# A decode block on one core: TensorE's code in four instruction blocks, VectorE and ScalarE in loops

## The chip, the core and the metric

The kernel runs on one core of one Trainium2 chip. The metric is device time in microseconds (us) of one execution; three runs of the kernel before have a median of 1309.22 us (1309.11 to 1309.62). A core has TensorE (PE in the tables: matrix products; its weight loads are PEld), VectorE (DVE), ScalarE (ACT), GpSimd (POOL) and SyncE (SP, which here only starts transfers), and 16 DMA engines that carry data between the chip's main memory and the core's on-chip memory.

## The reference

The reference is one transformer block that decodes one token for two sequences (B = 2). All numbers are fp32.

```
x: (2, 1, 512)                       k_cache, v_cache: (2, 32 heads, 8192, 128)
q = layernorm(x) @ wq                # wq 512 x 4096 -> 32 heads of 128
p = softmax(q . k_cache / sqrt(128)) # per sequence and head, over 8192 positions
h = x + (p . v_cache) @ wo           # wo 4096 x 512
out = h + (silu(n @ w_gate) * (n @ w_up)) @ w_down,  n = layernorm(h)   # 512 -> 1792 -> 512
```

The two caches are 268 MB each and every byte is used once, so some 565 MB have to be read for about 34 thousand numbers of activations.

## The kernel before, in words

The 64 pairs of a sequence and a head are worked through as 32 units (`U`) of two heads of one sequence. One unit has one K tile and one V tile of 128 partitions by 16384 numbers (8.39 MB): a head's 8192 positions lie over 64 partitions, 128 positions on each. There are two K slots (`kslot`) and one V slot (`vslot`).

For a unit, VectorE multiplies the K tile by the query in two halves (L456) and adds up over the head's 128 numbers (L465), which gives the scores; then it takes each partition's largest score (L473). TensorE turns that column into a row (L355), VectorE takes the largest per head (L409), TensorE spreads it, scaled and negative, over the partitions (L357, L358), ScalarE copies it (L416, `nb`) and computes the exponentials with their sums (L422), TensorE adds the sums over the partitions (L360), VectorE takes the reciprocal (L435). When V has landed, TensorE multiplies it by the probabilities (L365, 32 products in four groups of rows that run beside each other), ScalarE scales and copies (L437, L442), and TensorE and ScalarE bring the unit's result into `oT` (L377, L444). The steps of unit i-1 stand in VectorE's program between the two halves of unit i.

SyncE starts all loads from one list, in order: `wq` (into the V slot), K0 in two halves, K1, V0, K2, V1, K3, and so on, then `wo`, `w_gate`, `w_up` and `w_down` into slots that have come free. A load that overwrites a slot waits until the slot's reader is done (`after`, `freed`): V0 waits for the last product on `wq`, K(i+2) for unit i's sums, V(i+1) for the products on V(i). A load that waits holds up those behind it in the list.

The queries come ahead of the first unit: `xb` holds each normalised input number 64 times, so that a product with 64 columns of weights leaves the query on 64 partitions; 8 groups of products (L328) go by turns into two banks and ScalarE copies each into `qsb` (L339). VectorE's first unit needs the first group alone.

TensorE's 31 first rounds are one loop (`Fori`, L384); VectorE's and ScalarE's programs are written out, unit by unit. TensorE's instructions are fetched in blocks by DMA. At the start TensorE makes a tour: it jumps to `stop1` (L215), and from each of five stops, which stand in different places of its program, to the next (L222) and at last back to `toured`; in the ordinary run each stop is jumped over (L219). After the last unit come `wo`, the second layernorm, gate and up products (L550), the residual (L569: each of four groups of 32 rows of one bank, `f_ps`, begins with a quarter of h), two products whose result nobody reads (L596), and 14 chunks of `w_down`, four products of 128 columns each, added to those four groups (L607). VectorE and ScalarE copy half of the bank each, and two transfers store the result (L634).

Of the kernel before, what the change touches and what calls it, by code (L numbers as in the profile page):

```python
# [5 lines left out]
OP = mybir.AluOpType  # L6
AX = mybir.AxisListType
PE = mybir.EngineType.PE

# [43 lines left out]
def decode_block(nc, x, k_cache, v_cache, wq, wo, w_gate, w_up, w_down, out):  # L53
# [38 lines left out]
    nscale = sbuf("nscale", 1, HP)  # L92
# [5 lines left out]
    om = sbuf("om", P, B, H, NQ)  # L98
# [4 lines left out]
    xT = sbuf("xT", P, DC, B)  # L103
# [21 lines left out]
    nb_ps = bank[0][:, P : P + 1]  # L125
# [12 lines left out]
    s_k = [g.sem(f"k{n}") for n in range(2)]  # L138

# [72 lines left out]
    STOPS = 5  # L212

    def tour(e):
        e.br("stop1")  # L215
        nc.switch_bb("toured", parent=None)

    def place_stop(e, n):
        e.br(f"past{n}")  # L219
        with nc.body(f"stop{n}", parent=None, valid_engines=[PE]):  # L220
            e.nop()
            e.br(f"stop{n + 1}" if n < STOPS else "toured")  # L222
        nc.switch_bb(f"past{n}")

    def stop(n):
        g.steps["tensor"].append(lambda e: place_stop(e, n))
# [22 lines left out]
    do("vector", lambda e: e.tensor_reduce(quarter, ident.rearrange("p (q r) -> p q r", q=NQ), axis=AX.X, op=OP.add))  # L249
    do("vector", lambda e: e.memset(opart, 0.0))  # L250
# [30 lines left out]
    for t, value in (  # L281
# [24 lines left out]
    wait("vector", p)  # L306
    p = do("vector", lambda e: e.tensor_copy(xT, yt), s_dve)  # L307
    wait("vector", p)
    xb = osb.rearrange("p (c m) -> p c m", c=DC * B)
    xb_done = do(  # L310
        "vector",
        lambda e: e.tensor_copy(xb, xT.rearrange("p c b -> p (c b)")[:, :, None].to_broadcast([P, DC * B, HP])),  # L312
        s_dve,
    )
    wait("tensor", xb_done, landed[("wq", 0), 0])
    wqv = vslot.rearrange("p (c m k d) -> p c k m d", c=DC, k=2, d=DH)
    q_done = []
    for n, (m, b) in enumerate((m, b) for m in range(0, MQ, 4) for b in range(B)):
        ps = wide[n % 2].rearrange("p (j d) -> p j d", d=DH)
        if n == 7:  # L320
            stop(1)
        if n > 1:
            wait("tensor", q_done[n - 2])
        for c in range(DC):
            for k in range(2):
                p = do(
                    "tensor",
                    lambda e, ps=ps, c=c, k=k, m=m, b=b: e.matmul(  # L328
                        ps[HALF[k]],
                        xb[:, c * B + b, :],  # L330
                        wqv[:, c, k, m : m + 4, :],
                        start=(c == 0),
                        stop=(c == DC - 1),
                    ),
                    s_pe if c == DC - 1 and k == 1 else None,
                )
        wait("scalar", p)
        q_done.append(
            do("scalar", lambda e, ps=ps, m=m, b=b: e.activation(qsb[:, b, m : m + 4, :], ps, AF.Copy), s_act)  # L339
        )  # L340
    freed["wq", 0] = p
    wait("tensor", consts_done)


    ROUND = 5
    base = g.count[s_pe]

    def at(i, n):
        return s_pe, base + ROUND * i + n

    MROW, NB, DEN, PV, OT = range(1, ROUND + 1)

    def pe_scores(e):
        e.wait_ge(s_dve_pe, 1)
        e.matmul(mrow, m1, ident, start=True, stop=True).then_inc(s_pe, 1)  # L355
        e.wait_ge(s_dve_pe, 2)
        e.matmul(nb_ps[HALF[0]], nscale, gm[:, 0:1], start=True, stop=True)  # L357
        e.matmul(nb_ps[HALF[1]], nscale, gm[:, 1:2], start=True, stop=True).then_inc(s_pe, 1)  # L358
        e.wait_ge(s_act_pe, 1)
        e.matmul(den, sides.rearrange("p w a -> p (w a)"), rs, start=True, stop=True).then_inc(s_pe, 1)  # L360

    def pe_values(e, t_v):
        for w in range(NW):
            t = w % 4
            inst = e.matmul(  # L365
                opart[32 * t : 32 * t + 2 * W, :],
                pz[:, w, :],
                t_v[:, w * W * DH : (w + 1) * W * DH],
                start=(w < 4),
                stop=(w >= NW - 4),  # L370
            )
        inst.then_inc(s_pe, 1)

    def pe_outputs(e):
# [5 lines left out]
        inst.then_inc(s_pe, 1)  # L380

    def pe_rounds(e):
# [9 lines left out]
        place_stop(e, 2)  # L392
# [6 lines left out]
    g.count[s_pe] = at(U - 1, OT)[1]  # L399


    def k_view(i, j0, n):
        return kslot[i % 2][:, j0 * DH : (j0 + n) * DH].rearrange("p (j d) -> p j d", d=DH)

    def biggest(i):
        wait("vector", at(i, MROW))
        do(
            "vector",
            lambda e: e.tensor_reduce(gm, mrow.rearrange("p (k r) -> p k r", k=2), axis=AX.X, op=OP.max),  # L409
            s_dve_pe,  # L410
        )

    def softmax(i):
        s = scores[i % 2]
        wait("scalar", at(i, NB))
        wait("scalar", do("scalar", lambda e: e.activation(nb, nb_ps, AF.Copy), s_act))  # L416
        if i == 0:
            wait("scalar", consts_done)
        for k, h in enumerate(HALF):
            do(  # L420
                "scalar",
                lambda e, k=k, h=h: e.activation(  # L422
                    pz[h, :, k * W : (k + 1) * W],
                    s[h].rearrange("p (w a) -> p w a", a=W),
                    AF.Exp,
                    bias=nb[h],
                    scale=SCALE,
                    accum_out=rs[h],
                ),
                s_act_pe if k else None,  # L430
            )

    def recip(i):
        wait("vector", at(i, DEN))
        p = do("vector", lambda e: e.reciprocal(r, den), s_dve)  # L435
        wait("scalar", p)
        do("scalar", lambda e: e.activation(rdiag, diag, AF.Copy, scale=r))  # L437

    def outputs(i):
        m, b = divmod(i, B)  # L440
        wait("scalar", at(i, PV))
        do("scalar", lambda e: e.activation(osb, opart, AF.Copy), s_act_pe)  # L442
        wait("scalar", at(i, OT))
        return do("scalar", lambda e: e.activation(oT[:, 2 * m : 2 * m + 2, b], ot_ps, AF.Copy), s_act)  # L444

    oT_done = {}
    for i in range(U):
        m, b = divmod(i, B)
        parts = 2
        n = NJ // parts  # L450
        wait("vector", q_done[m // 4 * B + b])
        for c in range(parts):
            wait("vector", landed[("k", i), c if i == 0 else 0])
            kt = k_view(i, c * n, n)
            qb = qsb[:, b, m, :][:, None, :].to_broadcast([P, n, DH])
            mult = do("vector", lambda e, kt=kt, qb=qb: e.tensor_tensor(kt, kt, qb, op=OP.mult), s_dve)  # L456
            if i and c == 0:
                biggest(i - 1)
                softmax(i - 1)
            if i and c == 1:  # L460
                recip(i - 1)
            wait("vector", mult)
            p = do(
                "vector",
                lambda e, kt=kt, s=scores[i % 2][:, c * n : (c + 1) * n]: e.tensor_reduce(s, kt, axis=AX.X, op=OP.add),  # L465
                s_dve,
            )
        freed["k", i] = p
        if i:
            oT_done[i - 1] = outputs(i - 1)  # L470
            freed["v", i - 1] = at(i - 1, PV)
        wait("vector", p)
        do("vector", lambda e, s=scores[i % 2]: e.tensor_reduce(m1, s, axis=AX.X, op=OP.max), s_dve_pe)  # L473
    biggest(U - 1)
    softmax(U - 1)
    do("scalar", lambda e: e.activation(warm, mhalf[:1, :], AF.Sigmoid))
    recip(U - 1)

    zeroed = do("vector", lambda e: e.memset(wide[0], 0.0), s_dve)
    oT_done[U - 1] = outputs(U - 1)
    freed["v", U - 1] = at(U - 1, PV)
    stop(3)
    wait("vector", oT_done[U - 1])
# [21 lines left out]
    wait("tensor", p, zeroed)  # L508
    for c in range(H):
# [54 lines left out]
    stop(4)  # L564
    wait("tensor", h1_done)
    for t in range(4):
        do(
            "tensor",
            lambda e, t=t: e.matmul(  # L569
                f_ps[32 * t : 32 * t + 32, :], place, h1[:, COLS[t] * P : (COLS[t] + 1) * P], start=True, stop=False  # L570
            ),
        )
# [22 lines left out]
    for _ in range(2):  # L595
        do("tensor", lambda e: e.matmul(opart[:32], hT[:, 0, :], osb, start=True, stop=True))  # L596
    wait("tensor", p)
    for c in range(FB):
        if c == 10:
            stop(5)  # L600
# [3 lines left out]
        for t in range(4):  # L604
# [3 lines left out]
                    f_ps[32 * t : 32 * t + 32, :],  # L608
                    gT[:, c * 32 : (c + 1) * 32],
                    wd_t[:, c * D + COLS[t] * P : c * D + (COLS[t] + 1) * P],  # L610
                    start=False,
                    stop=(c == FB - 1),
                ),
                s_pe if c == FB - 1 and t == 3 else None,
            )
    res = rest[:HP, : 2 * P]
# [68 lines left out]
```

## Time and profile before

| | |
|---|---|
| median of three runs | 1309.22 us |
| profiled execution, its own time | 1309.27 us |
| its span (first to last instruction) | 1307.9 us |
| busy: VectorE, TensorE, ScalarE | 1131.1, 433.6, 80.5 us |
| read from main memory | 564.66 MB, 432 GB/s over the span |

The profile's page gives busy time by engine, the span in 40 slices, the DMA queues, and the chain of work that ended last: from the last instruction back to whatever released it, step by step. Such a chain names one reason for each stretch; whether something else would have taken its place has to be read from the stretch itself. Times in the lists of instructions count from the span's start.

### The profile page before, as it was taken

What the parts mean: (1) busy time and instruction counts of PE and PEld (TensorE: products, weight loads), DVE (VectorE), ACT (ScalarE), POOL (GpSimd) and SP (SyncE); (2) the same over time, 40 slices, a digit from 0 to 9 for tenths busy, and PEclk for the clock granted to TensorE, in tenths of its full rate; (3) what the DMA queues carried; (4) which work ended last, traced back from release to release, by engine and by line L of the source; (5) the groups of instructions that cost most, each with busy time, mean ns of one, the idle gap of its engine ahead of it and who ended that gap; (6) DMA issues with size and microseconds to landing.
All of it is one profiled execution on the core that took longest, in us unless ns stands there. A gap on an engine that the chain in (4) does not pass through costs nothing.

```text
span 1307.9 us, 6728 instructions
## 1 busy us (share of the span) xinstructions
PE 433.6 (33%) x2956; PEld 135.5 (10%) x2956; DVE 1131.1 (86%) x246; ACT 80.5 (6%) x272; POOL 3.1 (0%) x15
## 2 busy tenths in 40 slices
PE   1733223333212333322333322333331233332166
PEld 0210001011000011000101100101100010110022
DVE  0999988889888889988888988888998888998841
ACT  0100000000000000000000000000000000000010
POOL 0000000000000000000000000000000000000000
PEclk9965566666566666556666655666665666665689
DMA  9999999999999999999999999999999999999998
GB/s 400 438 439 431 435 435 439 433 433 437 429 437 429 437 429 441 429 439 431 441 433 433 437 429 437 429 439 431 437 429 441 431 437 435 431 437 431 435 423 377
DMA packets 10965, 564.79 MB, mean 432 GB/s; under 512 B 1222, under 2 KB 1226, under 8 KB 1612
## 3 DMA queue, kind: packets, MB, share of 16 engines
q1 hardware_dynamic: 10948, 564.67, 99.7%
q8 instruction: 5, 0.08, 0.0%
q14 instruction: 4, 0.03, 0.0%
q10 hardware_dynamic: 8, 0.01, 0.0%
HBM read 564.66 MB, written 0.00 MB: 432 GB/s over the span
## 4 chain that ended last, share of the span: by engine, by line
DMA 51%; DVE 45%; issue 2%; PE 1%; POOL 0%; SPq 0%; ACT 0%; POOLq 0%; DVEq 0%
DMA kslot<-in_A_k_cache_dram 45%; DVE kslot L456 22%; DVE s L465 22%; DMA kslot<-in_A_v_cache_dram 3%; DMA kslot<-in_B_w_down_dram 3%; PE opart L365 1%; PE wide L328 0%; DVE gm L409 0%; DVE r L435 0%; SPq L627 0%; PE bank L607 0%; PE bank L273 0%; ACT qsb L339 0%; DVE ln_stats L255 0%; POOL ln_rstd L261 0%
## 5 line engine op out<-in xcount | busy, mean ns | idle before, releaser
L456 DVE TENSOR_TENSOR kslot<-kslot,qsb 128x8192 f32<-128x8192 f32 x64 | 555.6, 8681 | 106.4 <-DMA kslot<-in_A_k_cache_dram 99.7
L465 DVE TENSOR_REDUCE s<-kslot 128x64 f32<-128x8192 f32 x64 | 555.2, 8675 | 0.1
L365 PE MATMUL opart<-vslot,pz 128*8 128x512 f32 x1984 | 285.3, 740 | 243.3 <-DMA vslot<-in_A_v_cache_dram 243.3
L357 PE MATMUL bank<-gm,nscale 1*64 1x1 f32 x64 | 11.8, 250 | 357.0 <-DVE gm L409 357.0
L365 PEld LDWEIGHTS opart<-vslot,pz 128*8 128x8 f32 x1984 | 55.5, 104 | 447.0 <-DMA vslot<-in_A_v_cache_dram 245.9
L355 PE MATMUL bank<-ident,m 128*1 128x128 f32 x64 | 18.8, 396 | 165.5 <-DVE m L473 165.5
L357 PEld LDWEIGHTS bank<-gm,nscale 1*64 1x64 f32 x64 | 9.0, 199 | 373.0 <-DVE gm L409 373.0
L377 PE MATMUL bank<-rdiag,osb 128*128 128x2 f32 x256 | 34.5, 257 | 28.2 <-ACT osb L442 28.2
L437 ACT ACTIVATE rdiag<-fold,r 128x8 f32<-128x8 f32 x32 | 9.6, 300 | 484.6 <-DVE r L435 484.6
L416 ACT ACTIVATE nb<-bank 128x1 f32<-128x1 f32 x32 | 5.5, 171 | 547.6 <-PE bank L358 547.6
L377 PEld LDWEIGHTS bank<-rdiag,osb 128*128 128x128 f32 x256 | 31.8, 195 | 57.8 <-ACT osb L442 57.8
L360 PE MATMUL bank<-rs,sides 128*128 128x1 f32 x64 | 18.8, 363 | 41.5 <-ACT pz L422 41.5
L328 PE MATMUL wide<-vslot,osb 128*64 128x512 f32 x128 | 30.1, 634 | 0.7 <-DVE osb L312 0.7
L422 ACT ACTIVATE pz<-s,nb 64x128 f32<-64x128 f32 x64 | 25.5, 399 | 1.4
L442 ACT ACTIVATE osb<-opart 128x512 f32<-128x512 f32 x32 | 19.1, 596 | 70.2 <-PE opart L365 70.2
L360 PEld LDWEIGHTS bank<-rs,sides 128*128 128x128 f32 x64 | 16.1, 313 | 44.2 <-ACT pz L422 44.2
L355 PEld LDWEIGHTS bank<-ident,m 128*1 128x1 f32 x64 | 2.7, 81 | 169.0 <-DVE m L473 169.0
L307 DVE COPY xT<-bank 128x8 f32<-128x8 f32 x1 | 0.2, 166 | 22.0 <-PE bank L273 22.0
L422 ACT ACTIVATION_READ_ACCUMULATOR pz<-s,nb 64x1 f32 x64 | 11.8, 185 | 0.0
L358 PE MATMUL bank<-gm,nscale 1*64 1x1 f32 x64 | 11.8, 251 | 0.0
L255 DVE BATCH_NORM_STATS2 ln_stats<-attn 2x6 f32<-2x512 f32 x1 | 0.7, 686 | 12.7 <-PE attn L529 12.7
L328 PEld LDWEIGHTS wide<-vslot,osb 128*64 128x64 f32 x128 | 9.5, 147 | 20.5 <-issue 19.7
(65 smaller groups left out, 103.5 us busy)
## 6 DMA issues: line engine op xcount, KB each, us to landing
kslot<-in_A_k_cache_dram SPq DMA_DIRECT2D x2, 4096.0 KB, 37.0
vslot<-in_A_wo_dram SPq DMA_DIRECT2D x1, 5120.0 KB, 23.0
kslot<-in_B_w_gate_dram SPq DMA_DIRECT2D x1, 3584.0 KB, 31.6
kslot<-in_B_w_up_dram SPq DMA_DIRECT2D x2, 1792.0 KB, 37.4
vslot<-in_A_wo_dram SPq DMA_DIRECT2D x1, 3072.0 KB, 29.9
kslot<-in_B_w_down_dram SPq DMA_DIRECT2D x2, 1024.0 KB, 30.8
kslot<-in_B_w_down_dram SPq DMA_DIRECT2D x1, 768.0 KB, 33.3
kslot<-in_B_w_down_dram SPq DMA_DIRECT2D x1, 512.0 KB, 34.1
```

The source lines that it names most:

```text
L328: lambda e, ps=ps, c=c, k=k, m=m, b=b: e.matmul(ps[HALF[k]], xb[:, c * B + b, :], wqv[:, c, k, m : m + 4, :], start=(c == 0), stop=(c == D ...
L355: e.matmul(mrow, m1, ident, start=True, stop=True).then_inc(s_pe, 1)
L357: e.matmul(nb_ps[HALF[0]], nscale, gm[:, 0:1], start=True, stop=True)
L358: e.matmul(nb_ps[HALF[1]], nscale, gm[:, 1:2], start=True, stop=True).then_inc(s_pe, 1)
L360: e.matmul(den, sides.rearrange("p w a -> p (w a)"), rs, start=True, stop=True).then_inc(s_pe, 1)
L365: inst = e.matmul(opart[32 * t : 32 * t + 2 * W, :], pz[:, w, :], t_v[:, w * W * DH : (w + 1) * W * DH], start=(w < 4), stop=(w >= NW - 4),)
L377: inst = e.matmul(ot_ps, osb[:, a * DH : (a + 1) * DH], rdiag[:, a::W], start=(a == 0), stop=(a == W - 1))
L422: lambda e, k=k, h=h: e.activation(pz[h, :, k * W : (k + 1) * W], s[h].rearrange("p (w a) -> p w a", a=W), AF.Exp, bias=nb[h], scale=SCALE ...
L437: do("scalar", lambda e: e.activation(rdiag, diag, AF.Copy, scale=r))
L442: do("scalar", lambda e: e.activation(osb, opart, AF.Copy), s_act_pe)
L456: mult = do("vector", lambda e, kt=kt, qb=qb: e.tensor_tensor(kt, kt, qb, op=OP.mult), s_dve)
L465: lambda e, kt=kt, s=scores[i % 2][:, c * n : (c + 1) * n]: e.tensor_reduce(s, kt, axis=AX.X, op=OP.add),
```

## The change

TensorE's tour has two stops: `stop1` right behind the loop, and `stop2` ahead of the last part of `w_down`. From `stop2` a conditional jump that is always taken goes back to `toured`, with a hint given at the tour's start; a second hinted jump at the end of the program goes to `back`, beside `stop1`, and from there to `end`. VectorE and ScalarE run 15 rounds of two units in a loop, the units at both ends are written out, and the semaphores are counted back each round. VectorE marks a K slot free with `s_kfree`; a V slot is free (`s_vfree`) when ScalarE has written the unit's `oT`, where it was the last product on V.

The first tables show TensorE's program from its start to its loop: tour, transposes of the layernorm, query products. Before:

```order
L215 UNCONDITIONAL_BRANCH
L273 MATMUL bank<-ident,ln_y 128x2 x4
L328 MATMUL wide<-vslot,osb 64x512 x56
L219 UNCONDITIONAL_BRANCH
L222 UNCONDITIONAL_BRANCH
L328 MATMUL wide<-vslot,osb 64x512 x8
```

And now, where `picks` is a matrix of ones and zeros that VectorE makes at the start, and `osb` and `qsb` hold the products as ScalarE copied them:

```order
L222 BRANCH_PREFETCH_HINT
L223 UNCONDITIONAL_BRANCH
L297 MATMUL bank<-ident,ln_y 128x2 x4
L343 MATMUL wide<-vslot,hT 32x512 x32
L365 MATMUL bank<-osb,picks 128x512 x4
L365 MATMUL bank<-qsb,picks 128x512 x4
```

64 products of 64 rows have become 32 of 32 rows for both sequences at once, in four groups of rows beside each other and two banks (16 products each), and 8 products that spread one sequence's query over the partitions. The first query is ready when the first of the 8 is done and copied, and it stands behind all 32.

The next tables show what SyncE's first loads wait for (`pe`, `dve`, `kfree`, `vfree` are semaphores). Before:

```order
L627 DMA kslot1<-in_A_k_cache_dram 128x16384
L627 DMA vslot<-in_A_v_cache_dram 128x16384 [waits pe]
L627 DMA kslot0<-in_A_k_cache_dram 128x16384 [waits dve]
L627 DMA vslot<-in_A_v_cache_dram 128x16384 [waits pe]
L627 DMA kslot1<-in_A_k_cache_dram 128x16384 [waits dve]
```

And now:

```order
L700 DMA kslot1<-in_A_k_cache_dram 128x16384
L700 DMA vslot<-in_A_v_cache_dram 128x16384 [waits pe]
L700 DMA kslot0<-in_A_k_cache_dram 128x16384 [waits kfree]
L700 DMA vslot<-in_A_v_cache_dram 128x16384 [waits vfree]
L700 DMA kslot1<-in_A_k_cache_dram 128x16384 [waits kfree]
```

The order is the same; the second load of V (V1) now waits for ScalarE's last step of unit 0.

The last tables show TensorE's program from the up products to its end. Before:

```order
L550 MATMUL wide<-kslot,hT 32x448 x16
L596 MATMUL opart<-osb,hT 32x512 x2
L607 MATMUL bank<-kslot 32x128 x40
L219 UNCONDITIONAL_BRANCH
L222 UNCONDITIONAL_BRANCH
L607 MATMUL bank<-kslot 32x128 x16
```

And now:

```order
L591 MATMUL wide<-kslot,hT 32x448 x16
L654 MATMUL bank<-kslot 32x512 x8
L636 MATMUL bank<-kslot 32x128 x12
L238 UNCONDITIONAL_BRANCH
L241 COMPARE_AND_BRANCH
L673 MATMUL bank<-osb,fold 32x128 x4
L636 MATMUL bank<-kslot 32x128 x12
L685 COMPARE_AND_BRANCH
```

The two products that nobody reads are gone, the first 8 chunks of `w_down` are one product of 512 columns each, and a jump (L238) and four products that add these in (L673) stand between the landing of chunks 11 and 12 and their products.

The diff, cut to its core:

```diff
     def tour(e):
+        never["reg"] = e.alloc_register("never")
+        e.reg_mov(never["reg"], 0)
+        hint = e.mark_branch_hint_location()
         e.br("stop1")
+        never["hint"] = hint
         nc.switch_bb("toured", parent=None)
+    def stops(e):
+        e.br("past1")
+        with nc.body("stop1", parent=None, valid_engines=[PE]):
+            e.nop()
+            e.br("stop2")
+        with nc.body("back", parent=None, valid_engines=[PE]):
+            e.nop()
+            e.br("end")
+        nc.switch_bb("past1")
+    def far_stop(e):
+        e.br("past2")
+        with nc.body("stop2", parent=None, valid_engines=[PE]):
+            e.nop()
+            e.br_lt(never["reg"], 1, "toured", "past2").branch_hint(never["hint"])
+        nc.switch_bb("past2", parent=None)
...
+    raws = (osb, qsb[:, B - 1, MQ - 4 :, :].rearrange("p m d -> p (m d)"))
+    for pair, raw in enumerate(raws):
+        ps = wide[pair]
         for c in range(DC):
+            for t in range(4):
...
+                        ps[32 * t : 32 * t + 32, :],
+                        hT[:, c, :],
+                        wqv[:, c, t % 2, 8 * pair + 4 * (t // 2) : 8 * pair + 4 * (t // 2) + 4, :],
...
+        wait("scalar", p)
+        told.append(do("scalar", lambda e, ps=ps, raw=raw: e.activation(raw, ps, AF.Copy), s_act))
+    for n in range(8):
...
+            lambda e, o=o, b=b, pair=pair, ps=ps: e.matmul(
+                ps,
+                picks[:, o, b, :],
+                raws[pair],
...
+    freed["wq", 0] = wqv_read
...
-        e.matmul(mrow, m1, ident, start=True, stop=True).then_inc(s_pe, 1)
+        e.transpose(mrow, m1, ident).then_inc(s_pe_dve, 1)
...
-        e.matmul(nb_ps[HALF[0]], nscale, gm[:, 0:1], start=True, stop=True)
-        e.matmul(nb_ps[HALF[1]], nscale, gm[:, 1:2], start=True, stop=True).then_inc(s_pe, 1)
+        e.matmul(nb_ps, nscale, gm, start=True, stop=True).then_inc(s_pe_act, 1)
...
+    def dve_rounds(e):
+        dve_unit(e, 0, qsb[:, 0, 0:1, :], True, 0, 0)
+        e.wait_ge(*q_done[-1])
+        e.sem_inc(s_own_dve, -4)
+        with nc.Fori(0, U // 2 - 1, engines=[DVE]) as m:
+            dve_unit(e, 1, qsb[:, 1, bass.ds(m, 1), :], False, 0, 0)
+            dve_unit(e, 0, qsb[:, 0, bass.ds(m + 1, 1), :], False, 4, 2)
...
+        dve_unit(e, 1, qsb[:, 1, U // 2 - 1 : U // 2, :], False, 0, 0)
...
+    def outputs(e, o, told, seen):
+        e.wait_ge(s_dve_act, told)
+        e.activation(rdiag, diag, AF.Copy, scale=r)
+        e.wait_ge(s_pe_act, seen)
+        e.activation(osb, opart, AF.Copy).then_inc(s_act_pe, 1)
+        e.wait_ge(s_pe_act, seen + 1)
+        e.activation(o, ot_ps, AF.Copy).then_inc(s_vfree, 1)
+    def act_rounds(e):
+        with nc.Fori(0, U // 2 - 1, engines=[ACT]) as m:
...
+        freed["k", i] = (s_kfree, i + 1)
+        freed["v", i] = (s_vfree, i + 1)
-            freed["v", i - 1] = at(i - 1, PV)
...
+    early = bank[2]
     wait("tensor", h1_done)
+    do("tensor", lambda e: e.matmul(early[:32, :], place, h1, start=True, stop=False))
...
-    for _ in range(2):
-        do("tensor", lambda e: e.matmul(opart[:32], hT[:, 0, :], osb, start=True, stop=True))
...
+            if c == EARLY - 1:
+                wait("scalar", p)
+                early_done = do("scalar", lambda e: e.activation(osb, early, AF.Copy), s_act)
+            continue
+        if c == WD[3][0]:
+            g.steps["tensor"].append(far_stop)
+            wait("tensor", early_done)
...
+    def last(e):
+        e.br_lt(never["reg"], 1, "back", "end").branch_hint(never["back"])
+        nc.switch_bb("end", parent=None)
```

## Rows read from the trace of the kernel before

**Rows 1.** The page: GB/s by slice, instruction queues (packets, MB), the chain by engine.

```profile
GB/s 400 438 439 431 435 435 439 433 433 437 429 437 429 437 429 441 429 439 431 441 433 433 437 429 437 429 439 431 437 429 441 431 437 435 431 437 431 435 423 377
...
q8 instruction: 5, 0.08, 0.0%
q14 instruction: 4, 0.03, 0.0%
...
DMA 51%; DVE 45%; issue 2%; PE 1%; POOL 0%; SPq 0%; ACT 0%; POOLq 0%; DVEq 0%
```

**Rows 2.** The chain in order of time, units 4 and 5: start, duration, what.

```profile
178.47 8.69 DVE kslot L456
...
213.28 42.43 DMA kslot<-in_A_k_cache_dram
...
255.74 8.69 DVE kslot L456
```

**Rows 3.** TensorE's jumps from stop to stop; its wait at the start.

```profile
L222 PEldq COMPARE_BRANCH  x5: 181/6042/7582, 1.2 to 25.7; - x5
```

**Rows 4.** DMA share by window at the start: us, clock, share of 16 engines, GB/s.

```profile
0.00:1.70 1.70, 1.00 0.00 1
...
1.80:1.90 0.10, 1.00 12.46 3953
```

**Rows 5.** DMA: load of wq to landing (us); queue 8 in 0:60; in 2.3:2.4.

```profile
vslot<-in_A_wq_dram SPq DMA_DIRECT2D x1, 23.2
...
q8 instruction: 5, 0.08, 0.5%
...
q8 instruction: 1, 0.02, 59.1%
```

**Rows 6.** Timeline of the first units: start, duration, engine, what, idle before.

```profile
0.74 0.41 SPq L627 DMA_DIRECT2D vslot<-in_A_wq_dram  x1
...
33.53 0.60 ACT L339 ACTIVATE qsb<-wide 128x512 f32<-128x512 f32 x1 [30.93 <-PE wide L328]
...
34.16 8.69 DVE L456 TENSOR_TENSOR kslot<-kslot,qsb 128x8192 f32<-128x8192 f32 x1 [6.78 <-ACT qsb L339]
...
57.56 0.33 SPq L627 DMA_DIRECT2D vslot<-in_A_v_cache_dram  x1
...
91.51 0.33 SPq L627 DMA_DIRECT2D vslot<-in_A_v_cache_dram  x1
...
98.05 0.17 ACT L444 ACTIVATE oT<-bank 128x2 f32<-128x2 f32 x1 [1.96 <-PE bank L377]
...
120.55 8.97 PE L365 MATMUL opart<-vslot,pz 128*8 128x512 f32 x64 [5.21 <-DMA vslot<-in_A_v_cache_dram]
```

**Rows 7.** The chain again: the first 16 query instructions on TensorE.

```profile
27.44 6.07 PE wide L328 x16
```

**Rows 8.** Timeline of the end, TensorE and its weight loads.

```profile
1273.08 4.47 PE L516 MATMUL wide<-vslot,oq 128*2 128x512 f32 x40 [0.32 <-ACT oq L507]
...
1298.64 1.88 PE L596 MATMUL opart<-osb,hT 128*32 128x512 f32 x4
...
1305.12 0.38 PEld L607 LDWEIGHTS bank<-kslot 128*32 128x32 f32 x16 [0.66 <-DMA kslot<-in_B_w_down_dram]
...
1305.75 0.16 PEld L607 LDWEIGHTS bank<-kslot 128*32 128x32 f32 x8 [0.26 <-DMA kslot<-in_B_w_down_dram]
```

**Rows 9.** Windows at the end: us, TensorE busy (instructions), clock, DMA share, GB/s.

```profile
1276.00:1280.00 4.00, 1.55 (x16) 1.00 1.01 434
...
1289.00:1290.00 1.00, 1.00 (x8) 0.50 0.97 416
...
1303.50:1304.00 0.50, 0.14 (x5) 1.00 0.76 303
...
1305.00:1305.40 0.40, 0.28 (x12) 1.00 0.05 20
```

**Rows 10.** TensorE's jumps past a stop: duration min/median/max in ns.

```profile
L219 PEldq COMPARE_BRANCH  x5: 163/169/176, 49.6 to 1303.9; - x5
```

More of the change, by code (lines that the diff above doesn't have):

```diff
@@ new lines, in decode_block, with softmax @@
+    wait("vector", q_done[0])
+    g.steps["vector"].append(dve_rounds)
+    def softmax(e, b, own, seen):
+        s = scores[b]
+        e.wait_ge(s_pe_act, seen)
+        for k, h in enumerate(HALF):
+            inst = e.activation(nb[h], nb_ps[h, k : k + 1], AF.Copy)
+        inst.then_inc(s_own_act, 1)
+        e.wait_ge(s_own_act, own)
+        for k, h in enumerate(HALF):
+            inst = e.activation(
+                pz[h, :, k * W : (k + 1) * W],
+                s[h].rearrange("p (w a) -> p w a", a=W),
+                AF.Exp,
+                bias=nb[h],
+                scale=SCALE,
+                accum_out=rs[h],
+            )
+        inst.then_inc(s_act_pe, 1)
@@ L482, in decode_block @@
+    wait("scalar", consts_done)
+    g.steps["scalar"].append(act_rounds)
+    for i in range(U):
+        freed["k", i] = (s_kfree, i + 1)
+        freed["v", i] = (s_vfree, i + 1)
     zeroed = do("vector", lambda e: e.memset(wide[0], 0.0), s_dve)
[L483 to L486, printed above, removed]
+    oT_done = freed["v", U - 1]
+    wait("vector", oT_done)
     p = do(
@@ L508, in decode_block @@
     wait("tensor", p, zeroed)
+    g.steps["tensor"].append(lambda e: never.update(back=e.mark_branch_hint_location()))
     for c in range(H):
@@ L594, in decode_block, with down @@
     p = do("vector", lambda e: e.transpose(gT, gu), s_dve)
-    for _ in range(2):
-        do("tensor", lambda e: e.matmul(opart[:32], hT[:, 0, :], osb, start=True, stop=True))
     wait("tensor", p)
+    EARLY = WD[2][0]
+    def down(c, t, first):
+        return do(
+            "tensor",
+            lambda e: e.matmul(
+                f_ps[32 * t : 32 * t + 32, :],
+                gT[:, c * 32 : (c + 1) * 32],
+                wd_t[:, c * D + COLS[t] * P : c * D + (COLS[t] + 1) * P],
+                start=first,
+                stop=(c == FB - 1),
+            ),
+            s_pe if c == FB - 1 and t == 3 else None,
+        )
     for c in range(FB):
-        if c == 10:
-            stop(5)
         for e_, (c0, n) in enumerate(WD):
@@ L603, in decode_block @@
                 wait("tensor", landed[("wd", 0), e_])
-        for t in range(4):
+        if c < EARLY:
+            t = c % 4
             p = do(
```

238 lines of the change are left out of this document (111 added, 127 removed).

## Prediction

> **What bounds the kernel now.** I read the page first: its slices show 423 to 441 GB/s from the second to the last but one, and its chain gives DMA 51% and VectorE 45% [rows 1]. A chain puts a transfer down to whatever it followed, so I read it in order of time, to see which of the two waits. In the steady stretch VectorE works on a unit from 178.47 to 213.28, that is 34.81 us, and then waits; two units come round every 255.74 - 178.47 = 77.27 us [rows 2]. In that time two K tiles and two V tiles come, 4 x 8.39 MB, so 434 GB/s: the transfers set the pace, and VectorE has 77.27 - 2 x 34.81 = 7.65 us to spare per two units. TensorE and ScalarE are busy less still. So the time is: when the stream of loads begins, its 564.66 MB, every hole in it, and what follows the last landing. The change touches no load. What it can move is the holes, the instruction fetches that travel on the same DMA engines, and the tail of about 2 us.
>
> The stream begins about 1.06 us after the first issue (issued at 0.74, nothing up to 1.7, all engines at work from 1.8 [rows 4, 6]). It doesn't end at once: the DMA share falls to 0.76 from 1303.5 on and is still 0.05 after 1305.0 [rows 9]. So the engines end up to 1.9 us apart, though each carries the same bytes. Five instruction fetches, all in the first 60 us, and four smaller ones later are the candidates [rows 1, 5]: one fetch of TensorE's holds one of 16 engines for 0.591 x 16 x 0.1 = 0.95 us [rows 5]; the four of 8 KB are, at 434/16 = 27 GB/s, an estimated 0.3 us each.
>
> **The loops and the fetches.** VectorE's and ScalarE's code shrinks from 32 written-out units to a loop of two, so the four later fetches go. TensorE's tour makes two stops in place of five. Its five jumps from stop to stop took 181 to 7582 ns, the first at 1.2 and the last at 25.7 [rows 3]; with one slow jump, or two, TensorE is ready by 5 to 13 us and not at 26. How many fetches remain the trace can't say: one to four of five. Since the stream ends with its latest engine, and one late engine is enough, fewer fetches give between nothing and the whole 1.9 us. I take -0.4: one of the small fetches on top of a large one no longer makes one engine latest of all, while one large one still does.
>
> What a round of a loop costs the trace of before shows on TensorE alone: 31 rounds, and no fetch after the first 60 us. The worst jump there, 7.58 us [rows 3], once per round of two units would still fit into VectorE's 7.65 us. So I take nothing for the loops' jumps; without that cover each microsecond over 7.65 would cost 15 us over the 15 rounds.
>
> [...]
>
> **The queries.** TensorE's first product on wq started at 27.44, though wq had landed at 0.74 + 23.2 = 23.9 [rows 5, 6, 7]. Now it starts at 23.9, or up to 0.95 earlier if one fetch less delays wq. Then: the first bank has 8 steps, each of four matmul instructions beside each other, as the old first group had 8 steps of two; that took 6.07 us from a cold start [rows 7]. The second bank's 8 steps at 4.47 us for 10 steps of the same width [rows 8] are 3.5 us. Then one spreading product of two passes over 512 columns, 1.0 us (two such steps and their drain), and ScalarE's copy, 0.60 [rows 6]. Sum: 23.9 + 6.1 + 3.5 + 1.0 + 0.6 = 35.1, against 34.16 for VectorE's first unit before [rows 6]. So VectorE starts 0 to 1.0 us later; I take +0.7 and 0.1 for entering its loop. The 3.5 us are saved and given back: the first query stands behind all 32 products. V0's issue, which waits for wq's last reader, moves from 57.56 [rows 6] to about 34 and is hidden: wq, K0 and K1 are 25.2 MB and keep the engines at work until 1.8 + 25.2/0.434 = 59.8.
>
> **The one place where a hole can open: V1.** V1's load now waits for ScalarE's last step of unit 0. Before, it was issued at 91.51, right behind the products on V0; that last step ended at 98.05 + 0.17 = 98.22, late because the reciprocal stands in VectorE's program behind the second half of unit 1 [rows 6]. With VectorE 0.8 later, V1 is issued at 99.0 (98.2 to 99.4) and its first bytes move 1.06 later, at 100.1. Is the queue empty by then? V1 landed at 120.5, when the products on it began [rows 6], so its last engine began it at 120.5 - 8.39/0.434 = 101.2, and by the 1.9 us of spread the first one at 99.3. So the early engines now run dry for up to 0.8 us and the late ones don't notice. A hole that only the early engines have costs nothing: it evens them out. There may be a charge for starting all engines afresh: wq took 23.2 from issue to landing, where 1.06 + 19.3 make 20.4; of the other 2.8 the spread explains 1.9, so up to 0.9. V1 then lands at 119.4 to 120.7, against 120.5. I take -0.2. In the steady stretch nothing of this is near: V(i) lands 19.3 us after unit i+1 began, its products take 9.0 [rows 6], and the next V is needed after 38.6; 10.3 us are left, more than the 6.7 by which the wait moved here (98.22 - 91.51).
>
> **The tail.** The change puts a jump and four products between the landing of chunks 11 and 12 and their products. A jump past a stop takes 0.17 us [rows 10]; four products are 8 instructions, 0.19 us at 16 weight loads in 0.38 [rows 8]. Before, TensorE was idle 0.26 us ahead of the last chunk [rows 8]. So +0.36 - 0.26 = +0.1 us; between 0 (the last chunk lands later than that anyway) and 0.36. The wider products for chunks 0 to 7 end long before chunk 8 is there. The two unread products, 1.88 us from 1298.64 on [rows 8], filled a gap that is now empty. [...] But in the window 1276 to 1280, with 2.4 us without work, the granted clock stayed at 1.00 [rows 9]. I add nothing, and keep up to +0.9 for the range.
>
> **Sum.** The profiled execution took 1309.27 us, its span and 1.4 us around it; the median of the runs is 1309.22, so nothing has to be shifted. 1309.27 - 0.4 (fetches) - 0.2 (V1) + 0.1 (tail) = 1308.8 us. The bounds of the terms together: -1.9 to 0, -1.1 to +0.2, 0 to +1.3. The first two share the same 1.9 us of spread, so together -1.9: 1307.4 to 1310.8.
>
> **Rivals.** First, V1 comes too late for the late engines as well: if the queries take longer than I added up (the clock stays down through the second bank, +3.4 us), V1 starts near 103.5, 2.3 us after the last engine was free, and with the charge for a new start the time is 1309.3 + 2.3 + 0.9 - 0.4 = 1312.1. It decides from a V1 issue after about 100.1 on. For it: the first group did start cold; against it: its 8 steps took 6.07 us, less than the 7.2 of 8 steps at half the pace of 0.45, so the clock rose within them [rows 7, 8].
>
> Second, and slower too: a loop's block isn't kept and is fetched in each round. TensorE's 31 rounds at 0.95 us are 29.5 us of DMA engine time, 1.8 us if the fetches go round all 16 engines, 1311.1; if they fall on half of the engines it is 3.7 us, 1313. TensorE's old loop, which fetched nothing after the first 60 us [rows 1, 5], speaks against it.
>
> Third, faster: the spread goes completely, because the remaining fetches lie before V1's start and that evens all engines: the stream ends 1.9 us earlier, 1307.4. For it: exactly that start. Against it: the charge of up to 0.9.
>
> Fourth, nothing of this matters and the spread has another cause: 1309.3 + 0.1 = 1309.4.
>
> **How the numbers follow.** My forecast, the stream as it was with slightly less spread, 1308.8 (own range 1308.0 to 1309.6): 0.60. No difference at all, 1309.4: 0.15. Spread gone, 1307.4: 0.13. V1 late, 1312.1 at its full size, more likely half of it: 0.07. Fetch in each round: 0.05. So 8 in 10 lie between 1307.3 and 1310.3. A measurement of this kernel can tell about 0.2% from no change, that is 2.6 us: under 1306.6 I see no mechanism, 0.03; over 1311.8 half of the last two cases, 0.06; within, 0.91.
>
> **What would show it.** Right: 423 GB/s and more in every slice; VectorE's first unit near 35; V1 issued near 99 and landed near 120; no instruction packets on VectorE's and ScalarE's queue between 60 and 1300; the DMA share falling more steeply at the end; under 1.3 us from the last landing to the result's issue. Wrong: instruction packets in every round, a slice under 420 GB/s near 100, VectorE's units further apart than 77.3 per two, or the granted clock at 0.50 after 1300.

## The result, and the profile after

The changed kernel is slower: a median of 1311.17 us (1310.41 to 1312.12, 22 runs) against 1309.17 us of the kernel before on the same chips (1309.0 to 1310.78, 22 runs), a ratio of 1.0015 [1.0009, 1.0021], 2.0 us. The forecast was 1308.8 with a range up to 1310.3. The profiled execution took 1311.51 us, its span 1310.0, against 1309.27 and 1307.9. So its difference is 2.2 us, and the chain of waits can say where they arose.

The page after, in the lines that answer to [rows 1]:

```profile
GB/s 401 444 432 418 418 448 416 448 416 448 416 448 416 448 442 422 448 416 448 416 448 438 426 446 418 448 416 448 416 448 442 422 448 416 448 416 448 432 425 377
...
q8 instruction: 3, 0.05, 0.0%
q14 instruction: 2, 0.02, 0.0%
...
DMA 52%; DVE 45%; PE 2%; issue 0%; DVEq 0%; ACT 0%; SPq 0%
```

The bound is the same, and there are fewer instruction packets: 3 and 2 for 5 and 4. But the row of GB/s now swings between 416 and 448, where before it stayed between 429 and 441 through the middle; the swing is there from the fourth slice on, which is where V1 is loaded. That a slice near 100 lies under 420 (the fourth and the fifth, 418) was one of the prediction's signs of being wrong. The swing by itself is no sign of a loss, as the last section shows. No slice from there on is under 416 but the last, which was 377 before too.

The timeline of the first units after (start, duration, engine, what; in brackets idle before and what ended it), for [rows 6] and [rows 7]:

```profile
24.06 9.47 PE L343 MATMUL wide<-vslot,hT 128*32 128x512 f32 x64 [13.14 <-DMA vslot<-in_A_wq_dram]
...
33.59 0.33 SPq L700 DMA_DIRECT2D vslot<-in_A_v_cache_dram  x1
33.60 0.60 ACT L355 ACTIVATE qsb<-wide 128x512 f32<-128x512 f32 x1 [2.84 <-PE wide L343]
...
34.63 0.60 ACT L378 ACTIVATE qsb<-bank 128x512 f32<-128x512 f32 x1 [0.43 <-PE bank L365]
35.26 8.69 DVE L452 TENSOR_TENSOR kslot<-kslot,qsb 128x8192 f32<-128x8192 f32 x1 [24.13 <-ACT qsb L378]
...
96.56 0.15 DVE L441 RECIPROCAL r<-bank 128x1 f32<-128x1 f32 x1
...
99.72 0.17 ACT L503 ACTIVATE oT<-bank 128x2 f32 x1 [2.06 <-PE bank L411]
99.92 0.33 SPq L700 DMA_DIRECT2D vslot<-in_A_v_cache_dram  x1
...
121.86 4.48 PE L399 MATMUL opart<-vslot,pz 128*8 128x512 f32 x28 [4.60 <-DMA vslot<-in_A_v_cache_dram]
```

V1 is issued at 99.92, 8.41 us later than before, and the products on it begin at 121.86, 1.31 us later. The chain of waits (start, duration, what) says what became of this, to be read against [rows 2]:

```profile
179.95 8.69 DVE kslot L452
...
214.83 42.49 DMA kslot<-in_A_k_cache_dram
...
257.47 8.69 DVE kslot L452
```

Unit 4 begins 1.48 us later than before and unit 6 1.73 us. The copies of the result begin at 1308.36 against 1306.24, 2.12 later; so of the whole loss 1.3 us are there when V1 lands, 1.7 by the sixth unit, and the next thousand microseconds with all rounds of the loops add 0.1. The rest is in the tail, 0.27. V1's landing shows the last of 16 engines alone; how much the whole stream had lost by then is counted below.

### The profile page after: what moved, and what is told of

Its sections match the earlier page's. It is cut to its first block, busy times and chain, and to the rows that moved or that the text cites. A ratio compares the mean times of both kernels' runs of the same rounds, so it can differ in the third digit from the quotient of the medians.

```text
span 1310.0 us, 6657 instructions
## 1 busy us (share of the span) xinstructions
PE 421.5 (32%) x2762; PEld 136.3 (10%) x2762; DVE 1131.2 (86%) x247; ACT 87.7 (7%) x307; POOL 3.1 (0%) x15
## 4 chain that ended last, share of the span: by engine, by line
DMA 52%; DVE 45%; PE 2%; issue 0%; DVEq 0%; ACT 0%; SPq 0%
DMA kslot<-in_A_k_cache_dram 45%; DVE kslot L452 22%; DVE s L456 22%; DMA kslot<-in_A_v_cache_dram 3%; DMA kslot<-in_B_w_down_dram 2%; DMA vslot<-in_A_wq_dram 2%; PE opart L399 1%; PE wide L343 1%; DVE gm L437 0%; DVE r L441 0%; SPq L700 0%; PE bank L365 0%; PE bank L411 0%; DVEq L452 0%; PE bank L636 0%
## 5 line engine op out<-in xcount | busy, mean ns | idle before, releaser
L392 PE MATMUL bank<-gm,nscale 1*128 1x2 f32 x64 | 18.6, 358 | 360.5 <-DVE gm L437 360.5
L390 PE MATMUL bank<-ident,m 128*1 128x128 f32 x32 | 11.9, 373 | 190.6 <-DVE m L459 190.6
L392 PEld LDWEIGHTS bank<-gm,nscale 1*128 1x128 f32 x64 | 15.9, 306 | 369.9 <-DVE gm L437 369.9
L483 ACT ACTIVATE nb<-bank 64x1 f32<-64x1 f32 x64 | 10.6, 166 | 573.2 <-PE bank L392 572.8
L343 PE MATMUL wide<-vslot,hT 128*32 128x512 f32 x64 | 9.5, 758 | 13.1 <-DMA vslot<-in_A_wq_dram 13.1
L459 DVE TENSOR_REDUCE m<-s 128x1 f32<-128x128 f32 x32 | 9.1, 286 | 4.7
L557 PE MATMUL wide<-vslot,oq 128*2 128x512 f32 x64 | 9.8, 779 | 0.4 <-ACT oq L547 0.4
```

Source lines behind the costliest of these rows:

```text
L343: lambda e, c=c, t=t, ps=ps, pair=pair: e.matmul(ps[32 * t : 32 * t + 32, :], hT[:, c, :], wqv[:, c, t % 2, 8 * pair + 4 * (t // 2) : 8 * ...
L390: e.transpose(mrow, m1, ident).then_inc(s_pe_dve, 1)
L392: e.matmul(nb_ps, nscale, gm, start=True, stop=True).then_inc(s_pe_act, 1)
L483: inst = e.activation(nb[h], nb_ps[h, k : k + 1], AF.Copy)
L557: lambda e, c=c, t=t: e.matmul(wide[0][32 * t : 32 * t + B, :], oq[:, c, :], wo_t[:, c * D : (c + 1) * D], start=(c < 4), stop=(c >= H - 4),),
```

## The experiments

My theory once the result was seen: V1 is issued too late, the DMA engines run dry ahead of it, and the stream never gets this back. Rivals: VectorE's late start by itself (unit 0 began 1.10 us later), and the code (loops, jumps and fetches) or the tail. Each run below was timed in five rounds beside the kernel before (medians 1309.10 to 1309.15).

**v_free_early.** The changed kernel, but the V slot is marked free when the products on V are done, as it was before.

```
     def outputs(e, o, told, seen):
+        e.wait_ge(s_pe_act, seen)
+        e.sem_inc(s_vfree, 1)
         e.wait_ge(s_dve_act, told)
         ...
-        e.wait_ge(s_pe_act, seen)
-        e.activation(o, ot_ps, AF.Copy).then_inc(s_vfree, 1)
+        e.activation(o, ot_ps, AF.Copy).then_inc(s_ot, 1)
```

> The changed kernel, but a V slot is marked free as soon as ScalarE sees the last product on V, and not after the unit's last copy. Theory (a hole in the stream at V1, because V1's load is issued at 99.9, when the engines run dry between 99.5 and 101.2): V1 issued near 92, its last landing back from 121.8 to about 120.5, the time down by 1.3 to 1.6 us, to 1309.6 to 1309.9 or a ratio near 1.0004 to the kernel before. Rival (the loops, their jumps and fetches, or the tail cost the 2 us): unchanged, near 1311.2.

Median 1309.34 us (1308.90 to 1309.99), ratio 1.0001 [0.9992, 1.0010]. V1 was issued at 92.21. Everything else of the change was in it, VectorE's late reciprocal too (96.95, later still than after's 96.56). This one release gives back 1.8 of the 2.0 us, so what the loops, the jumps and VectorE's late start cost together is too small to be told. The edit moves the release in every unit, so it doesn't by itself tell V1 from a cost in each of the 32 units; that the loss is there by unit 6 and grows by 0.1 from there to the last landing does.

**before_v_late.** The other direction: the kernel before, with its V loads alone made to wait for `oT`.

```
-            freed["v", i - 1] = at(i - 1, PV)
+            freed["v", i - 1] = oT_done[i - 1]
```

> The kernel before with one edit: a V slot comes free only when the unit's result is copied, as in the changed kernel; no loops, old queries. V1 is issued near 98.25 and not at 91.5, first bytes near 99.3, just when the first engines run dry and 1.5 us before the last does. Theory (a hole at V1): 0 to +0.5 us against before, 1309.2 to 1309.7. Rival (the late release costs in each of 32 units): +2 us or more.

Median 1310.42 us (1309.49 to 1311.75), ratio 1.0010 [1.0001, 1.0020]. V1 was issued at 98.23, which is the lower end of what my prediction took for the changed kernel and held to be free, and it cost 1.3 us in the median, more than the 0 to 0.5 I had expected of it and less than the rival's 2. In the profiled execution (1309.89) products on V1 start only 0.22 later and unit 6 0.61, and at the last landing (1305.70 against 1305.07) it is 0.63: nothing is added in the units between.

**before_v_late_start_late.** The same, and VectorE's first unit waits for the second query group as well.

```
-        wait("vector", q_done[m // 4 * B + b])
+        wait("vector", q_done[max(1, m // 4 * B + b)])
```

> The kernel before with two edits: V comes free when the unit's result is copied, and VectorE's first unit waits for the second group of queries, so it starts near 37.6 (3.4 us later). V1 is issued near 101.7, first bytes near 102.7, 1.5 us after the last engine ran dry and 3.4 after the first. Theory (hole at V1, with a charge for starting all engines afresh): V1's last landing near 123 to 123.5, time +2.5 to +3.5 us, 1311.7 to 1312.7. Rival (the changed kernel's 2 us are its loops, fetches and tail; VectorE catches up by unit 4 anyway): within 0.5 us of the kernel before.

Median 1313.26 us (1311.39 to 1314.01), ratio 1.0029 [1.0019, 1.0040]. VectorE started at 37.18, V1 was issued at 101.26, its products began at 123.08, 2.53 us later than in the kernel before, and unit 6 at 259.74, 4.00 later. That is over the 1312.7 that I had put as the upper end. With the code of before and a later V1 it loses more than the changed kernel. So the time goes with V1's issue and not with the code. That the late start by itself does no harm is v_free_early's to show, which starts as late as the changed kernel.

What the DMA engines do around V1's issue is seen in the transfers by window (window, length, TensorE's clock, share of 16 engines, GB/s; a packet is counted where it begins). The kernel before:

```profile
97.00:99.00 2.00, 0.50 0.98 426
99.00:100.00 1.00, 0.50 1.67 721
100.00:101.00 1.00, 0.50 0.76 328
101.00:102.00 1.00, 0.50 0.76 328
```

The changed kernel:

```profile
97.00:99.00 2.00, 0.50 0.61 262
97.30:98.30 1.00, 0.50 0.00 0
98.50:100.80 2.30, 0.50 0.00 0
100.80:101.70 0.90, 0.50 3.43 1165
```

before_v_late, and behind it before_v_late_start_late:

```profile
97.00:99.00 2.00, 0.50 0.99 426
99.00:100.00 1.00, 0.50 1.76 655
...
101.00:102.00 1.00, 0.50 0.15 66
```

```profile
97.00:99.00 2.00, 0.50 0.60 262
99.00:100.00 1.00, 0.50 0.01 0
...
102.00:103.00 1.00, 0.50 3.15 1049
```

The figures go in steps of 0.066 MB, which is one packet. The time of one packet follows from a row too: share x window x 16 engines / packets. Before, 16 packets begin between 99 and 101 (11 and 5) and take 2.4 us each, so an engine with work begins one every 2.4 us. After, 8 begin between 97 and 99, six of them up to 97.30 and two from 98.30 on. Counted with one packet at a time for an engine (from 60 to 1300 the packets of the loads before take 100.1% of 16 engines' time), 14 of the 16 engines were done by 99.7 and two by 101. No packet begins from 98.50 to 100.80, and then all 16 engines begin one within 0.9 us. The 8 engines that began none from 97 on were done by 99.4: half of the engines stand still for 1.4 us at least, six more for 1.1, the last two for less.

Nor is that all: V1's first 16 packets take 3.09 us each (3.43 x 0.90 x 16 / 16) and not 2.4. In before_v_late_start_late nothing begins until 102, and then all 16 engines begin in one microsecond, with packets of 3.15 us. In before_v_late the rows shown differ little in number from the kernel before, one packet fewer from 99 to 100 and four fewer from 101 to 102, but the ten from 99 to 100 take 2.82 us each (1.76 x 16 / 10).

What the whole stream lost can be counted over a longer window, the kernel before first and the changed one behind it:

```profile
98.00:110.00 12.00, 0.50 1.01 437
```

```profile
98.00:110.00 12.00, 0.50 0.89 360
```

That is 80 packets before and 66 after. The 14 that are missing are 0.92 MB, 2.1 us of a stream of 434 GB/s, and the last landing of all is 1.86 us later than before: to a packet or two, all that the stream lost was lost within 10 us of V1's issue. V1's landing is only 1.31 us later because the last engine sets it, and the last two had lost least. before_v_late_start_late begins 53 packets in this window (289 GB/s); the 27 missing are 4.1 us, against 2.53 us at V1's landing and 4.00 at unit 6.

**queries_by_halves.** The changed kernel, with the four products that spread the first bank's queries put ahead of the second bank's products on wq, so that VectorE starts earlier.

```
-    for n in range(8):
-        o, b = divmod(n % 4, B)
-        pair, m = n // 4, 4 * (n // B)
+        for n in range(4 * pair, 4 * pair + 4):
+            o, b = divmod(n % 4, B)
+            m = 4 * (n // B)
```

> The changed kernel, but the four products that spread the first bank's queries stand ahead of the second bank's 16 products, so VectorE's first unit starts near 32.5 and not 35.3. V still comes free after the unit's last copy. Theory (hole at V1): everything in unit 0 and 1 moves 2.8 us earlier, V1 is issued near 97.1, first bytes near 98.1, before the first engine runs dry: 1309.6 to 1309.9. Rival (the late release itself costs in every unit): about 1311; rival (loops, fetches, tail): 1311.2.

Median 1310.27 us (1309.30 to 1311.36), ratio 1.0009 [1.0000, 1.0018], over the 1309.6 to 1309.9 expected. VectorE started at 33.92 and not sooner, since the first half of K0 landed only then:

```profile
33.92 8.69 DVE L452 TENSOR_TENSOR kslot<-kslot,qsb 128x8192 f32<-128x8192 f32 x1 [22.91 <-DMA kslot<-in_A_k_cache_dram]
```

So V1 was issued at 98.57 and not at the 97.1 I had expected. It lies between the changed kernel and the kernel before in cause and in time.

**v_early_tail_moved** and **v_early_tail_halves.** v_free_early, with the jump and the four products of the tail moved ahead of the wait for the last part of `w_down`; the second has the queries by halves as well.

```
     for c in range(FB):
+        if c == WD[3][0]:
+            g.steps["tensor"].append(far_stop)
+            wait("tensor", early_done)
+            for t in range(4):
+                do("tensor", lambda e, t=t: e.matmul(f_ps[32 * t : 32 * t + 32, :], fold,
+                    osb[:, COLS[t] * P : (COLS[t] + 1) * P], start=False, stop=False))
         for e_, (c0, n) in enumerate(WD):
         ...
-        if c == WD[3][0]:
-            g.steps["tensor"].append(far_stop)
-            wait("tensor", early_done)
         ...
```

> The changed kernel with V freed at the last product on V, and with the jump and the four products that add chunks 0 to 7 in moved ahead of the wait for chunks 11 and 12. The profile after shows 0.79 us from the last landing to the two last copies (1307.57 to 1308.36), the one before 0.53. Theory (jump and four products lie on the path): back to about 0.5 us, 0.2 to 0.3 us off v_free_early's 1309.34, so 1309.1. Rival (TensorE's clock or the missing unread products make the tail slower): no change, 1309.3.

> As v_early_tail_moved, with the queries spread by halves too, so VectorE's first unit starts 1.4 us earlier (K0's first half, landed at 33.8, bounds it) and V1 is issued near 90.9. Theory (V1 is late only near the point where the engines run dry): no difference to v_early_tail_moved, 1309.1. Rival (an earlier start of VectorE is worth something by itself): faster by up to 1 us.

Medians 1309.19 (1308.71 to 1309.90) and 1309.07 us (1308.76 to 1309.54), ratios 1.0000 [0.9991, 1.0009] and 0.9999 [0.9990, 1.0008]. The tail is worth 0.15 us in the median against v_free_early, less than can be told apart. In the second, products on V1 began at 121.11, no earlier than in queries_by_halves (121.10), and yet it ends 1.2 us earlier, of which the tail is 0.2 at most: a shift of half a microsecond in one load's landing proves no hole by itself, since the last of 16 engines sets it. The window from 98 to 110 does tell the two apart: 437 GB/s, as before, and 393.

**before_v_at_reciprocal** and **v_after_reciprocal.** Where does it begin to cost? The kernel before with V's load waiting for the unit's reciprocal too, and v_early_tail_moved with the slot marked free one step later, by the activation behind the reciprocal.

```
             freed["v", i - 1] = at(i - 1, PV)
+            also["v", i - 1] = told[i - 1]
         ...
             wait("sync", freed[after[item]])
+            if after[item] in also:
+                wait("sync", also[after[item]])
```

```
-        e.sem_inc(s_vfree, 1)
         e.wait_ge(s_dve_act, told)
-        e.activation(rdiag, diag, AF.Copy, scale=r)
+        e.activation(rdiag, diag, AF.Copy, scale=r).then_inc(s_vfree, 1)
```

> The kernel before, with the next V's load waiting for unit 0's reciprocal as well (in each unit), so V1 is issued near 95.3, 6 us before the last engine runs dry and 4 before the first. The other runs: issue at 91.5 takes 1309.1, at 98.2 1310.4, at 99.9 1311.2, at 101.3 1313.3. Theory (a cost only when an engine finds nothing queued): 1309.1 to 1309.2. Rival (the cost grows with a shorter queue even while nothing is dry): about 1309.8.

> v_early_tail_moved with V's release moved back to ScalarE's copy behind the reciprocal (rdiag), so V1 is issued near 97.1, between before_v_at_reciprocal (95.0: no cost) and before_v_late (98.2: +1.3 us). First bytes near 98.2, 1.3 us ahead of the first engine running dry at 99.5. Theory (a cost only once an engine finds nothing queued; a load needs 1.06 us from issue to first bytes): 1309.1 to 1309.3. Rival (a load must be queued some 3 us ahead, since the engines start it unevenly and slowly): 1309.5 to 1310.2.

Medians 1309.12 (1308.93 to 1309.56) and 1309.29 us (1308.81 to 1309.97), ratios 1.0000 [0.9991, 1.0009] and 1.0001 [0.9992, 1.0010]. All runs by V1's issue:

| V1 issued | to its landing | GB/s, 98 to 110 | kernel | median against before |
|---|---|---|---|---|
| 91.51 | 29.0 | 437 | before | 0 |
| 91.34 | 29.7 | 437 | v_early_tail_halves | -0.1 |
| 91.47 | 29.2 | 437 | v_early_tail_moved | 0.0 |
| 92.21 | 28.7 | 437 | v_free_early | +0.2 |
| 94.98 | 25.6 | 437 | before_v_at_reciprocal | 0.0 |
| 96.60 | 24.1 | 421 | v_after_reciprocal | +0.1 |
| 98.23 | 22.5 | 426 | before_v_late | +1.3 |
| 98.57 | 22.5 | 393 | queries_by_halves | +1.2 |
| 99.92 | 21.9 | 360 | after | +2.0 |
| 101.26 | 21.8 | 289 | before_v_late_start_late | +4.2 |

With either code, a V1 issued by 96.6 shows no cost that can be told from no change, and one issued from 98.2 on does. From 98.6 to 101.3 the time grows with the delay, and the missing bytes with it. The theory of a cost only once an engine finds nothing queued is not quite what the traces show: in v_after_reciprocal 13 packets begin between 99 and 100, two more than in the kernel before, so the engines hardly stand still there, and yet these packets take 2.98 us each (2.42 x 16 / 13).

```profile
99.00:100.00 1.00, 0.50 2.42 852
```

From 98 to 110 three packets are missing (77 for 80), 0.5 us, which the median doesn't show. In before_v_at_reciprocal, issued 1.6 us earlier, none are.

## Why the prediction was wrong, point by point

**What bounds the kernel** was right: the stream of loads, with holes in it as the one thing the change could move by much.

**The loops and the fetches.** The tour came out as described: one slow jump, and TensorE ready at 10.3, within the 5 to 13. The jumps after (duration min/median/max in ns, first and last start; L231 is from stop to stop), and TensorE's first products:

```profile
L231 PEldq COMPARE_BRANCH  x1: 8436/8436/8436, 1.4 to 1.4; - x1
```

```profile
10.32 0.61 PE L297 MATMUL bank<-ident,ln_y 2*128 2x2 f32 x4 [10.32 <-issue]
```

Nothing is fetched in the rounds of the loops: from 60 to 1230, when VectorE's and ScalarE's rounds are over, the trace has no instruction packet at all, and from there to 1308 two on q14, the queue that I put down to these two engines, where I had said none, and none on q8, which I put down to TensorE. So the rival of a fetch in each round did not come, over 15 rounds on two engines and 31 on a third.

The term for fewer fetches, -0.4, was not seen: v_free_early has the tour and the loops of the changed kernel and no gain, but its +0.2 has an interval of about 1.2 us either way, too wide to rule 0.4 out. My premise that one late engine is enough to hold the end would explain it, as two fetches on q8 still lie in the first 60 us, for five before; no run tests that.

**The queries.** The sum of 35.1 for VectorE's first unit was good: 35.26, and both banks took 9.47 us where I had 9.6. But I put +0.7 into the next step, against the +0.94 that this sum gives and +1.10 measured.

**The one place where a hole can open: V1.** This is the step that failed; its place was right and its size wrong. I took the term as -0.2, between -1.1 and +0.2; measured are +1.31 at V1's landing and 2.1 us of the stream by 110. It was wrong in two ways.

First, the issue: 99.92 instead of 99.0, and outside of my 98.2 to 99.4. VectorE starts 1.10 later and not 0.7 + 0.1; over the next two units 0.34 more is lost (96.56 - 35.26 = 61.30 from start to reciprocal, 60.96 before), which I put down to the loop's entry and the marking of slots, and ScalarE's and TensorE's steps behind the reciprocal take 3.33 instead of 3.10.

Second, the price of a hole. "A hole that only the early engines have costs nothing: it evens them out" does not hold, nor that the late ones don't notice. I had the first engine free at 99.3 and the last at 101.2, and let the late ones carry the stream; but 14 of 16 were done by 99.7. They stood still for 1.1 us at least, eight of them for 1.4, where I had up to 0.8, and the load landed 1.31 us later. The charge for a new start, "up to 0.9", is 1.4 to 1.5: V1's load in the changed kernel (engine, count, us from issue to landing)

```profile
vslot<-in_A_v_cache_dram SPq DMA_DIRECT2D x1, 21.9
```

took 21.9 us and in before_v_late_start_late 21.8, where 1.06 + 19.3 make 20.4. Of that charge 0.7 are V1's first packets, 3.09 us and not 2.4; the rest I put down to the engines beginning up to 0.9 us apart. With these, 99.92 + 21.9 = 121.8 is V1's landing, against the 120.3 of my taken values with the whole charge (99.0 + 20.4 + 0.9): 0.9 of the difference comes from the issue and 0.6 from the charge.

I also expected the evening out to end the stream more steeply, and it did (windows at the end, columns as in [rows 9] without TensorE's):

```profile
1305.00:1306.00 1.00, 1.00 1.03 418
1306.00:1307.00 1.00, 1.00 0.50 193
1307.00:1308.00 1.00, 1.00 0.02 6
```

The share goes from 1.03 to 0.02 within two microseconds, where before it fell from 1303.5 on and still was 0.05 after 1305.0 [rows 9]. But the last of them ends 1.86 us later: the narrower spread is no gain when the early engines have been held back, and the late ones with them.

**The rivals.** The first, V1 too late for the late engines as well, was the mechanism, and 1312.1 nearer to the 1311.2 measured than my forecast. It had a chance of 0.07 because I let it decide from an issue after 100.1 on, worked out from when the last engine is free. Measured, it decides between 96.6 and 98.2. What the rival started from, a TensorE that stays slow through the second bank, did not come: the weight loads for the first bank's steps begin 0.85 us apart up to 28.30, those for the second's 0.43 apart (29.49 to 32.49). The granted clock was 1.00 all the while, and so it was in the first group before (27.44 to 33.51), whose steps went from 0.85 to 0.43 us; what rose there was the pace, and no trace shows that the clock did. The third, the spread gone, 1307.4, had the hole right and its sign wrong.

**The tail.** +0.1 was priced, with 0 to 0.36 for the jump and the products; measured are 0.27 more from the last landing to the copies (2.12 - 1.86, the chain's last transfer ending at 1306.93 against 1305.07). Of these 0.24 lie ahead of the four products, which begin 0.28 us behind the landing, where the next products did 0.04 behind it before:

```profile
1305.74 0.86 PE L636 MATMUL bank<-kslot 128*32 128x128 f32 x24 [0.78 <-DMA kslot<-in_B_w_down_dram]
...
1307.21 0.43 PE L673 MATMUL bank<-osb,fold 128*32 128x128 f32 x8 [0.61 <-DMA kslot<-in_B_w_down_dram]
...
1307.46 0.84 PE L636 MATMUL bank<-kslot 128*32 128x128 f32 x24
...
1308.36 0.27 ACT L694 ACTIVATE kslot<-bank 64x128 f32<-64x128 f32 x1 [2.73 <-PE bank L636]
```

TensorE's granted clock was 1.00 here (1296 to 1310) in spite of the missing two products, as taken. No run shows the +0.9 that I kept for the range: in v_early_tail_moved, where the clock was 0.50 from 1302 to 1305, the products on chunks 8 to 10 took 0.65 us longer than here, and the copies came no later (last section).

**What stays open.** Three things. Why before_v_late costs 1.3 us in the median, when its profiled execution cost 0.6 and misses two packets from 98 to 110: its runs spread more (1309.49 to 1311.75 against 1308.93 to 1309.43), so the hole may differ from run to run, and one profile shows one of them. Then, what makes V1's first packets long, 2.82 to 3.15 us, in every run that issues V1 at 96.6 or later. And what sets the spread of the engines at the end; that each carries the same bytes, as I wrote, no trace shows, since none tells which engine took a packet. No version came out faster than the kernel before by more than a tenth of a microsecond.

## What to carry to other kernels

When a stream of loads sets the time, look for each load at the time from its issue to the moment when the engines have nothing else, and not only at whether it lands before it is needed. A slot that is handed back a few steps later cost next to nothing here in the steady state (0.1 us from unit 6 to the last landing) and yet opened a hole once, at the start, and that was kept to the end; an issue 2.7 us before the first engine was free (96.6 against my estimate of 99.3) was early enough and one of 1.1 us was not. And count the bytes over a window behind such a place: the landing of one load shows only its last engine. And where a sum gives a number, put that number into the next step: of the delay of V1 0.2 us came from rounding my own sum down.

## What the runs showed of the hardware

The loads went in waves in the changed kernel, as if its 16 engines ran in step, and that by itself cost nothing: v_early_tail_moved shows it too, at a ratio of 1.0000. By windows of 4 us, the transfers before lie near their mean; in the changed kernel they go by about 524, 508, 279, that is some two packets, two and one per engine, over and over. The kernel before, and behind it the changed one:

```profile
140.00:144.00 4.00, 0.50 1.06 459
144.00:148.00 4.00, 0.50 1.02 442
148.00:152.00 4.00, 0.50 0.94 410
```

```profile
140.00:144.00 4.00, 0.50 1.21 524
144.00:148.00 4.00, 0.50 1.17 508
148.00:152.00 4.00, 0.50 0.64 279
```

That goes with the swing of the page's GB/s, which lasts to the end of the span. It is not the hole that makes it: v_early_tail_moved, where V1 is issued at 91.47 and no time is lost, shows nearly the same:

```profile
140.00:144.00 4.00, 0.50 1.13 492
144.00:148.00 4.00, 0.50 1.21 524
148.00:152.00 4.00, 0.50 0.68 295
```

What makes the waves there no run tests.

And TensorE's granted clock fell in the tail of one run: in v_early_tail_moved it was 0.50 from 1302 to 1305, where each other run shows 1.00 (windows; columns: window, length, TensorE busy and count, weight loads, the other engines, clock, DMA share, GB/s).

```profile
1302.00:1303.00 1.00, 1.00 (x8) 0.01 (x2) 0.00 (x0) 0.00 (x0) 0.00 (x0) 0.50 1.01 412
...
1304.00:1305.00 1.00, 1.00 (x28) 0.92 (x24) 0.00 (x0) 0.41 (x1) 0.00 (x0) 0.50 0.14 53
1305.00:1306.00 1.00, 1.00 (x36) 0.84 (x28) 0.00 (x0) 0.00 (x0) 0.00 (x0) 0.90 0.01 4
```

The products on chunks 8 to 10 there (timeline, as above):

```profile
1303.68 1.51 PE L637 MATMUL bank<-kslot 128*32 128x128 f32 x24
```

They took 1.51 us, against 0.86 in the changed kernel. In the 4 us before, 1298 to 1302, TensorE had been busy for 1.9 us; in v_early_tail_halves it had been for 2.1 us, and the clock stayed at 1.00. Why it fell in the one and not in the other stays open. It was not paid for at the end: its copies began at 1306.21, against 1306.72 in v_free_early.
